# Attention into a mixture of experts: relu of k and a share of the v scaling on GpSimd, relu of q as one operation, a first block table of six batches

## The chip, the cores and the metric

The kernel runs on one core of one Trainium2 chip. Its time is device microseconds of one execution. The core has five engines that take instructions from queues of their own, each in order: TensorE (PE, whose weight loads are listed as PEld), VectorE (DVE), ScalarE (ACT), GpSimd (POOL) and SyncE (SP, which here only issues DMAs). Engines wait for each other by semaphores only.

## The reference

q, k and v are 8 batches x 8 heads x 576 tokens x 64, in float32. The attention is linear, so there is no 576 x 576 matrix; its output is the input of a mixture of 8 experts in which each token goes to one expert.

```python
phi(x) = concat(relu(x) * cos(theta), relu(x) * sin(theta))     # theta = pi/2 * pos / 576
kv  = einsum('bhsf,bhsd->bhfd', phi(k), v);  z = sum_s phi(k)
x   = (phi(q) @ kv) / (phi(q) @ z + 1e-6)                       # 4608 tokens x 512
e   = argmax(x @ w_gate);  gate = softmax(x @ w_gate)[e]
y   = relu(x_of_expert @ w1[e]) @ w2[e]                         # 512 -> 1024 -> 512, at most 1152 tokens an expert
out[token] = gate * y
```

## The kernel before

**Attention, batch by batch.** A batch is 576 tokens of 8 heads, held as two halves u of four heads. SP loads k, q (one transfer a half) and v. Relu of k is done in place (`relu_k`, L408 to L416: two ACT operations of 128x1152 a batch). Instead of scaling k by cos and sin, the kernel scales v (`scale_v`, L421 to L436): for each of nine position groups j and each of the two tables one operation of 128x256, those of odd j on ACT (8 a batch), those of even j on DVE (10 a batch). Relu of q (`q_relu`, L441 to L446) goes from the loaded layout (head, j, 64) to a layout in which PE can transpose two heads at a time (j, head, 64); it is four DVE operations of 128x576 a batch, one for each half and head of a pair. Then come, per batch:

- KV (L491, PE): 2 x 36 matmuls; needs relu of k and all 18 scaled v pieces.
- Q (L454, PE, three groups a half) with copies to SBUF by ACT (`rq`, L461).
- kvt (L503, ACT), T (L520, PE), tsb (L525, ACT), G (L534, PE), kva (L508 and L539, ACT): the gate weights are folded into KV, so that x @ w_gate comes out of the same matmuls as x.
- P (L561, PE): ten units a batch; each is followed by a copy (`tmp`, L568, ACT) and a scalar_tensor_tensor (`num`, L573, DVE). Three PSUM slots ("p") hold them.

**Routing of a batch.** A chain of some 20 small DVE operations (L614 to L722) finds each token's expert and gate; in the middle stands a group of small matmuls on PE (L680 to L687, called "count" below) that counts tokens, with a running sum (`carry`, L698) from batch to batch. Five pieces of the tokens (`xg`, L745; two on POOL, three on DVE) are scaled, cast to bf16 and scattered by POOL's indirect DMAs (L754, five a batch) into `xd` in DRAM, where each expert has a region.

**Block tables and the experts.** The experts work on 43 blocks of 128 rows of `xd`. Two tables say which expert and which row each block has. Table a (`tab_ops`, L784 to L892, some 18 DVE operations) is made from the carry after BA = 7 batches and holds the NA = 24 blocks that are certain to be full by then; table b holds the NB = 19 others, after batch 8. SP makes a small read of `xd` (`seen`, L1066) that waits for the scatters of the first BA batches; every fetch of a block (`xr`, L948) comes after it. Fetches of table b's blocks also wait for the last scatters and for eight DMAs of zeros that ACT issues (`pad`, L882). A block is: fetch, transpose by PE (L957), copy to `un` by DVE (L961), up-projection half 0 (L977, `w1a`), relu (L984, ACT), transpose (L992), copy (L998, DVE); later half 1 (`w1b`) the same way, and last the down-projection (L1018), a copy (L1024 ACT or L1026 DVE) and POOL's scatter to the output (L1035). PE's order is: all half-0 blocks, all half-1 blocks, all down blocks, with some mixing at the seams. Weights are loaded by POOL's DMAs (L899, L910); w1a during the attention, the others after `swap` has given the attention's memory to them.

**What sets the order.** A planner in the kernel (`Plan.schedule`, L87) takes each operation with an engine, a cost and a latency, and a priority to which the table `PHI` adds an offset by name. It makes one list; each engine gets its operations in that order and keeps to it, whatever happens on the chip. So a changed cost or offset moves instructions on all engines.

Of the kernel before, what the change touches and what calls it, by code (L numbers as in the profile page):

```python
# [27 lines left out]
    "G": -1.04, "KV": -0.66, "P": -0.87, "R": -0.81, "T": -0.03, "carry": 0.36, "down": -0.02, "end": 1.83,  # L28
    "gout": -0.99, "hT": -1.51, "ids": -0.3, "ix": 0.26, "kva": -0.29, "kvt": -1.41, "load": 0.03, "pad": 1.0,
    "pos": -0.09, "relu": 0.27, "reluk": -0.58, "reluq": -0.46, "rq": -0.61, "scat": 1.16, "tab": 1.94,  # L30
    "tmp": 0.1, "tsb": -2.25, "turn": -0.08, "up": 0.59, "vs": -1.24, "w1": 1.29, "w2": 1.39, "wg": 0.98,
    "xT": -0.23, "xg": 1.25, "xturn": 1.8, "y": 0.55,
# [141 lines left out]
def kernel(  # L174
# [30 lines left out]
    BA = 7  # L205
# [4 lines left out]
    U0, U1, U2 = 4, 41, 42  # L210

# [191 lines left out]
    def attention(b):  # L403
# [4 lines left out]
        def relu_k(u):  # L408
            def f():
                kk = loaded[b, "k", u].tile[:]  # L410
                nc.scalar.activation(out=kk, in_=kk, func=ACT.Relu)  # L411
            return f

        for u in range(2):
            op("ACT", 1.1, relu_k(u), r=[("k", b, u)], w=[("rk", b, u)], vers=[loaded[b, "k", u]], prio=pr - 0.4,
               ).tag = ("reluk", b, u)  # L416
# [4 lines left out]
        def scale_v(j, t):  # L421
            def f():
                tab = (cosn, sinn)[t]
                dst, src = vs_t[vs.slot][:, :, j, t, 0:D], vm.tile[:, :, j, :]
                if (j, t) in ON_ACT:
                    nc.scalar.activation(out=dst, in_=src, func=ACT.Copy, scale=tab[:, j:j + 1])
                else:
                    nc.vector.tensor_scalar(out=dst, in0=src, scalar1=tab[:, j:j + 1], scalar2=None, op0=ALU.mult)
            return f

        ON_ACT = {(j, t) for j in range(J) for t in range(2) if j % 2}
        for j in range(J):
            for t in range(2):
                act = (j, t) in ON_ACT
                op("ACT" if act else "DVE", 0.41 if act else 0.31, scale_v(j, t), r=[("v", b, 0), ("v", b, 1)],
                   w=[("vs", b, j)], vers=[vs, vm], prio=pr - 0.3).tag = ("vs", b, j, t)  # L436
# [4 lines left out]
        def q_relu(u, qr, c):  # L441
            def f():
                t = tl(qr, [P, J, 2, D], FP32, "early")
                nc.vector.tensor_scalar(out=t[:, :, c, :], in0=loaded[b, "q", u].tile[:, c, :, :], scalar1=0.0,  # L444
                                        scalar2=None, op0=ALU.max)
# [19 lines left out]
        for u in range(2):  # L465
            qr = Ver(qrS)
            for c in range(2):
                op("DVE", 0.38, q_relu(u, qr, c), r=[("q", b, u)], w=[("qr", b, u)], vers=[loaded[b, "q", u], qr],
                   prio=pr - 0.4).tag = ("reluq", b, u, c)
            for jq in range(3):  # L470
# [3 lines left out]
                op("PE", 0.11 * n, f, r=[("qr", b, u)], w=[("qps", b, u, jq)], vers=[pv, rq[u], qr], prio=pr,  # L474
                   mode="full").tag = ("Q", b, u, jq)
                op("ACT", 0.5 if n == 4 else 0.22, g, r=[("qps", b, u, jq)], w=[("rq", b, u)], vers=[pv, rq[u]],
                   prio=pr - 0.2).tag = ("rq", b, u, jq)
# [19 lines left out]
        for u in range(2):  # L497
            op("PE", 2.07, kv_half(u), r=[("rk", b, u)] + [("vs", b, j) for j in range(J)], w=[("kvps", b)],
               vers=[kv, kva, loaded[b, "k", u], vs], prio=pr, mode="quad").tag = ("KV", b, u)
# [11 lines left out]
        op("ACT", 0.52, kvt_out, r=[("kvps", b)], w=[("kvt", b)], vers=[kv, kvt], prio=pr - 0.5).tag = ("kvt", b)  # L511
        op("ACT", 0.53, kva_out, r=[("kvps", b)], w=[("kva", b)], vers=[kv, kva], prio=pr - 0.5).tag = ("kva", b)
# [30 lines left out]
        op("PE", 0.45, transp, r=[("kvt", b)], w=[("tps", b)], vers=[tv, tsb, kvt], prio=pr - 0.5, mode="full").tag = ("T", b)  # L543
# [607 lines left out]
```

## Time and profile before

| what | value |
|---|---|
| median of 3 runs (lowest, highest) | 405.65 us (404.07, 406.15) |
| the profiled execution, its span | 407.73 us, 406.0 us |
| busy: PE, DVE, ACT, POOL | 329.1, 215.0, 178.0, 143.3 us |
| attention on PE (first KV to last P) | 10.45 to 176.2 us |
| first up-projection | 197.72 us |
| first down-projection | 323.74 us |
| mean TensorE clock | 0.931 |

The profile page has the span in 40 slices of about 10.15 us, with a digit for the busy tenths of each engine, and the clock that TensorE was granted (PEclk). The stage table used below gives for each stretch its length and then each engine's busy us and instruction count in the order PE, PEld, DVE, ACT, POOL, and last the clock, the busy share of the DMA engines and GB/s. Group lines give: line, engine, operation, output and inputs with their shapes, count, busy us, mean ns, and what the engine waited for before them. Lines about one source line give the duration of one as shortest/median/longest in ns.

### The profile page before, as it was taken

The numbers are of one execution on the slowest core, as the hardware profiler recorded it, in microseconds if no ns is written. First come the engines' busy times: TensorE is split into PE (matmuls) and PEld (weight loads), VectorE is DVE, ScalarE is ACT, GpSimd is POOL, SyncE is SP. The second block draws the span as 40 slices with busy tenths as digits, with TensorE's granted clock in tenths as the row PEclk, the third lists the DMA queues.
The fourth block names the chain that finished last, engine by engine and source line by source line (L and its number), as shares of the span: only waits on it lengthen the run. The fifth ranks groups of instructions, "written<-read, shape, count | busy, mean of one in ns | idle before, by whom it ended". The sixth has DMA issues, their size and how long they took to land.

```text
span 406.0 us, 9624 instructions
## 1 busy us (share of the span) xinstructions
PE 329.1 (81%) x3333; PEld 218.0 (54%) x3356; DVE 215.0 (53%) x612; ACT 178.0 (44%) x369; POOL 143.3 (35%) x212
## 2 busy tenths in 40 slices
PE   0886788898969799830587779899999999999992
PEld 0776676687757588620344345555555544444440
DVE  7548988876938758789543344454333322222220
ACT  6359787866737653620132324334555411111110
POOL 3001627153441604575423211215000046556552
PEclk9989999969988959985599999999999999999997
DMA  8975979699680530529999995645960024433320
GB/s 293 360 284 184 329 260 307 199 269 254 194 241 19 178 52 16 98 69 189 219 193 231 193 197 123 140 115 94 210 114 0 2 105 155 152 149 129 136 104 10
DMA packets 39535, 66.63 MB, mean 164 GB/s; under 512 B 4927, under 2 KB 19647, under 8 KB 39490
## 3 DMA queue, kind: packets, MB, share of 16 engines
q0 software_dynamic: 18032, 30.96, 34.6%
q1 hardware_dynamic: 20306, 34.01, 25.3%
q10 hardware_dynamic: 1152, 1.05, 0.8%
q8 instruction: 29, 0.48, 0.5%
q14 instruction: 16, 0.13, 0.1%
HBM read 67.56 MB, written 17.06 MB: 208 GB/s over the span
## 4 chain that ended last, share of the span: by engine, by line
PE 51%; DVE 14%; issue 9%; DMA 8%; POOL 7%; ACT 7%; another core or an unknown queue 2%; POOLq 1%; SPq 0%; DVEq 0%; ACTq 0%
PE p L977 18%; PE p L1018 9%; PE p L561 9%; POOL out_dram L1035 5%; PE a L992 4%; PE a L454 3%; DMA wg_n<-in_moe_w_gate_dram 3%; DMA xr<-xd 2%; PE a L957 2%; DVE qr L444 2%; DVE xg L745 2%; PE p L491 2%; PE a L534 2%; DVE num L573 2%; DMA km<-in_k_dram 2%
## 5 line engine op out<-in xcount | busy, mean ns | idle before, releaser
L984 ACT ACTIVATE h<-p 128x512 bf16<-128x512 f32 x86 | 51.3, 597 | 92.8 <-PE p L977 55.4
L1018 PE MATMUL p<-w,un 128*128 x337 | 74.2, 379 | 0.4
L998 DVE COPY un<-a 128x512 bf16<-128x512 bf16 x86 | 36.2, 423 | 62.4 <-PE a L992 62.1
L561 PE MATMUL p<-kva,rq 64*128 64x146 f32 x640 | 58.6, 326 | 8.0 <-DVE num L573 5.1
L561 PEld LDWEIGHTS p<-kva,rq 64*128 64x128 f32 x640 | 49.2, 212 | 15.3 <-DVE num L573 7.1
L573 DVE SCALAR_TENSOR_TENSOR num<-p,tant,tmp 128x292 f32<-128x292 f32 (+1 forms) x80 | 39.2, 512 | 33.6 <-ACT tmp L568 29.5
L1018 PEld LDWEIGHTS <-un 128*128 128x128 bf16 x344 | 33.6, 98 | 40.3 <-issue 0.4
L491 PE MATMUL p<-vs,km 64*64 64x130 f32 x1152 | 41.0, 286 | 14.7 <-ACT km L411 12.2
L977 PEld LDWEIGHTS <-un 128*128 128x128 bf16 x344 | 32.6, 98 | 33.7 <-issue 8.8
L754 POOL DMA_INDIRECT xd<-xg,si x40 | 42.9, 1074 | 21.4 <-DVE xg L745 12.3
L977 PE MATMUL p<-w1a,un 128*128 x162 | 44.1, 392 | 7.0 <-DVE un L961 4.4
L568 ACT COPY tmp<-p 128x292 f32<-128x292 f32 (+1 forms) x80 | 31.4, 401 | 33.3 <-PE p L561 21.3
L1026 DVE COPY y<-p 128x512 f32<-128x512 f32 x22 | 15.2, 691 | 57.7 <-PE p L1018 46.0
L491 PEld LDWEIGHTS p<-vs,km 64*64 64x64 f32 x1152 | 35.8, 141 | 18.6 <-issue 14.8
L1035 POOL DMA_INDIRECT out_dram<-y,ids x24 | 23.6, 982 | 60.2 <-issue 60.2
L977 PE MATMUL p<-w1b,un 128*128 x166 | 43.3, 377 | 0.4
L992 PEld LDWEIGHTS <-h 128*128 128x128 bf16 x344 | 25.2, 98 | 26.2 <-ACT h L984 10.5
L1024 ACT COPY y<-p 128x512 f32<-128x512 f32 x21 | 12.3, 585 | 60.9 <-PE p L1018 57.9
L992 PE MATMUL a<-identb,h 128*128 128x128 bf16 x344 | 33.1, 220 | 6.0 <-ACT h L984 3.5
L957 PE MATMUL a<-identb,xr 128*128 128x128 bf16 x172 | 17.5, 227 | 14.9 <-DMA xr<-xd 11.6
L454 PE MATMUL a<-ident,qr 128*128 128x128 f32 x144 | 26.7, 313 | 2.1 <-ACT rq L461 0.9
L952 POOL COPY ids<-xr 128x2 bf16<-128x2 bf16 x43 | 7.8, 189 | 57.7 <-DMA xr<-xd 57.4
(157 smaller groups left out, 384.4 us busy)
## 6 DMA issues: line engine op xcount, KB each, us to landing
vm<-in_v_dram SPq DMA_DIRECT2D x16, 576.0 KB
km<-in_k_dram SPq DMA_DIRECT2D x16, 576.0 KB
qm<-in_q_dram SPq DMA_DIRECT2D x16, 576.0 KB
w<-in_moe_w_dram POOLq DMA_DIRECT2D x16, 512.0 KB
xr<-xd SPq DMA_DIRECT2D x43, 128.5 KB
w1a<-in_moe_w_dram POOLq DMA_DIRECT2D x8, 512.0 KB
w1b<-in_moe_w_dram POOLq DMA_DIRECT2D x8, 512.0 KB
xd<-zrow ACTq DMA_DIRECT2D x8, 128.5 KB
```

What stands on the lines that cost most here:

```text
L454: nc.tensor.transpose(out=q_ps[:, n * P:(n + 1) * P], in_=qr.tile[:, j, :, :].rearrange("p c d -> p (c d)"), identity=ident[:])
L491: nc.tensor.matmul(out=kv_v[c * D:(c + 1) * D, o, u, :, :], lhsT=loaded[b, "k", u].tile[o * D:(o + 1) * D, c, j, :], rhs=vs_t[vs.slot][o * ...
L561: nc.tensor.matmul(out=p_ps[:, a, o, 0:2 * KW], lhsT=rq[u].tile[a * D:(a + 1) * D, o, col:col + P], rhs=kva.tile[a * D:(a + 1) * D, o, u, ...
L568: nc.scalar.copy(out=t[0:rows], in_=p_v[0:rows, :, 0:KW])
L573: nc.vector.scalar_tensor_tensor(out=num.tile[0:rows, c, u * HB:(u + 1) * HB, :], in0=p_v[0:rows, :, KW:2 * KW], scalar=tant[0:rows, c:c + ...
L754: si = nc.gpsimd.indirect_dma_start(out=xd[:, :], out_offset=bass.IndirectOffsetOnAxis(ap=xg.si[0:rows, c:c + 1], axis=0), in_=xg.tile[0:r ...
L977: nc.tensor.matmul(out=hp, lhsT=xv.tile[:, g, :], rhs=w1h[m][:, bass.ds(e1, 1), g, :], start=(g == 0), stop=(g == G - 1))
L984: nc.scalar.activation(out=h[:], in_=pvs[m].tile[:, 0, :].rearrange("p (g q i) -> p g i q", g=2, i=2), func=ACT.Relu)
L992: nc.tensor.transpose(out=t_ps[:, x * P:(x + 1) * P], in_=hvs[m].tile[:, x // 2, x % 2, :], identity=identb[:])
L998: nc.vector.tensor_copy(out=unit(hts[m])[:].rearrange("p f s -> p (f s)"), in_=tvs[m].tile[:].bitcast(BF16)[:, 0:512])
L1018: nc.tensor.matmul(out=y_ps, lhsT=hts[x // G].tile[:, x % G, :], rhs=w2h[x // G][:, bass.ds(e2, 1), x % G, :], start=(x == 0), stop=(x == ...
L1035: oi = nc.gpsimd.indirect_dma_start(out=out[:, :], out_offset=bass.IndirectOffsetOnAxis(ap=idx, axis=0), in_=yv.tile[:], in_offset=None, b ...
```

## The change

1. Relu of k goes from ACT to POOL (16 operations of 128x1152; `tensor_scalar` with max).
2. Of the v scaling, j = 4 and j = 8 go from DVE to POOL (32 operations of 128x256); DVE keeps six a batch, ACT its eight.
3. Relu of q is one DVE operation for each half (16 in all, in place of 32): it reads 2 x 9 x 64 in the loaded order and writes to the same target layout, the head as outermost dimension.
4. BA = 6 in place of 7, so table a has 20 blocks and table b 23. Three scratch tiles of the two tables (`sq`, `ge`, `gm`) become shared.
5. For the first 14 blocks the copy after the fetch's transpose goes from DVE to ACT (`XT_ACT`).
6. The w1a loads are released earlier: load e after KV of batch 3e/4, where it was e + 1.
7. The planner's costs, latencies and the whole table `PHI` are new.

```diff
 PHI = {
...
+    "G": 8.78, "KV": 6.99, "P": -1.6, "R": 1.52, "T": -0.09, "down": -0.82, "fetch": -0.06, "hT": -0.31,
...
-    BA = 7
+    BA = 6
...
+    XT_ACT = 14
...
-                nc.scalar.activation(out=kk, in_=kk, func=ACT.Relu)
+                nc.gpsimd.tensor_scalar(out=kk, in0=kk, scalar1=0.0, scalar2=None, op0=ALU.max)
...
+                    eng = nc.vector if where == "DVE" else nc.gpsimd
+                    eng.tensor_scalar(out=dst, in0=src, scalar1=tab[:, j:j + 1], scalar2=None, op0=ALU.mult)
...
-        ON_ACT = {(j, t) for j in range(J) for t in range(2) if j % 2}
+        def vs_on(j, t):
+            return "ACT" if j % 2 else "POOL" if j in (4, 8) else "DVE"
...
-                nc.vector.tensor_scalar(out=t[:, :, c, :], in0=loaded[b, "q", u].tile[:, c, :, :], scalar1=0.0,
-                                        scalar2=None, op0=ALU.max)
+                nc.vector.tensor_scalar(out=t[:].rearrange("p j c d -> p c j d"), in0=loaded[b, "q", u].tile[:],
+                                        scalar1=0.0, scalar2=None, op0=ALU.max)
...
+            if name not in T and name in ("sq", "ge", "gm"):
+                if name not in wide:
+                    m = E if name == "sq" else max(NA, NB)
+                    wide[name] = late.tile([P, m, shape[2]], dt, name=name)
+                T[name] = wide[name][:, 0:shape[1], :]
...
-            nc.vector.tensor_copy(out=unit(xv)[:].rearrange("p g s -> p (g s)"),
-                                  in_=xpv.tile[:].bitcast(BF16)[:, 0:DT])
+            dst, src = unit(xv)[:].rearrange("p g s -> p (g s)"), xpv.tile[:].bitcast(BF16)[:, 0:DT]
+            if i < XT_ACT:
+                nc.scalar.copy(out=dst, in_=src)
+            else:
+                nc.vector.tensor_copy(out=dst, in_=src)
...
-        w1_load(0, e, e + 0.1, ops_of("KV", min(e + 1, B - 1)))
+        w1_load(0, e, e + 0.1, ops_of("KV", 3 * e // 4))
```

## The prediction

> **What bounds the kernel now.** I read the slices of the page first, for where PE stands still, then the table by stage, then the timeline of the standstill, then PE's waits inside the attention.
>
> ```profile
> PE   0886788898969799830587779899999999999992
> PEclk9989999969988959985599999999999999999997
> 25.00:176.30 151.30, 127.85 (x1962) 107.50 (x1959) 115.59 (x313) 101.80 (x236) 59.93 (x66) 0.92 0.63 182
> 176.30:197.70 21.40, 1.79 (x23) 1.28 (x23) 18.91 (x69) 0.63 (x2) 15.12 (x21) 0.58 0.84 180
> 197.70:204.80 7.10, 6.87 (x31) 3.62 (x32) 1.70 (x4) 1.79 (x3) 0.64 (x3) 0.60 1.00 187
> 204.80:270.00 65.20, 52.98 (x415) 30.25 (x422) 28.09 (x84) 22.09 (x37) 15.09 (x48) 1.00 0.86 176
> 323.70:399.00 75.30, 74.26 (x341) 33.78 (x347) 15.81 (x24) 12.72 (x22) 41.15 (x42) 1.00 0.34 127
> ```
>
> From 204.8 us on PE works nearly all the time, and 75.3 us at the end are down-projections at full rate: nothing in the change touches them. There are two places to gain. The first is the hole at 176.3 us: 21.4 us with PE busy 1.8. The timeline shows what fills it: table a's 18 operations on DVE (182.67 to 187.87, for batch 8's routing comes first), the read "seen" (188.66), the first fetch (189.72), its transpose, and ACT's zero DMAs beside it.
>
> ```profile
> 188.66 0.33 SPq L1069 DMA_DIRECT2D seen<-xd  x1
> 191.39 7.92 ACTq L882 DMA_DIRECT2D xd<-zrow  x8
> 192.07 0.61 PE L957 MATMUL a<-identb,xr 128*128 128x128 bf16 x4 [11.05 <-DMA xr<-xd]
> ```
>
> The second is the attention. The counts of the routing (L680) start at 38.66, 59.31, 77.80, 104.51, 128.78, 152.33 and 167.59 us: 6 intervals of 21.5 us a batch. In the row from 25 to 176.3, PE is idle for 151.3 - 127.85 = 23.4 us, and the clock of 0.92 costs about 0.08 x 151.3 = 12 us more: 3.3 and 1.7 us a batch, which leaves 16.5 us of PE work. The idle time has these owners:
>
> ```profile
> PE p L561 <- DVE num L573: 5.1, 6, 1.7
> PE a L534 <- ACT tsb L525: 4.3, 5, 2.6
> PE a L520 <- ACT kvt L503: 2.8, 2, 2.4
> PE p L491 <- ACT km L411: 1.7, 1, 1.7
> ```
>
> All are late copies on DVE and ACT. The two longest (2.4 us at 117, 2.6 us at 142) stand beside the stretches in which PEclk falls to about half.
>
> **The hole (items 4, 6, 7).** In the built program's order, table a now stands on DVE right behind the sixth count, and PE still has, from that count to the last P: 20 P (1.26 us for two: 12.6), two KV halves (2.23 each: 4.5), T 0.66, two G (2.2), six Q groups (2.4), a count (0.6): 23 us. The other path from the same count: table 5 us (its time now), rest of the routing 2.3, POOL's two xg pieces 2.06, five scatters of 1.28 apart (6.4), landing 2.7, "seen" 1.0, fetch and landing 2.4: 22 us. They tie; I take 1.5 us of waiting for the first fetch in place of 21.4.
>
> What is late next: the eight zero DMAs took 7.92 us of ACT in the hole, at no cost. In the new order they stand in ACT's queue behind the fifth relu of the experts and ahead of the eighth copy of item 5 (`un7`) and the sixth relu. They wait for the eighth count, which itself comes a num (0.5), three xg pieces (2.0) and nine DVE operations (3.1 us) after the last P. PE has five up blocks by then (5 x 1.3 = 6.5 us, plus the start), and three or four things after; ACT is busy till about 17 us after the last P. Cost: 7 us of idle PE, plus about 3 us of low clock after it (the row at 0.60 shows four blocks in 7.1 us where 1.3 us each do, start to start, at 254 to 262 us). That low clock at the start, 3 us, is gone now, since PE comes straight from the attention. Sum: -21.4 + 1.5 + 7 + 3 - 3 = **-13 us**, between -19 (the zero DMAs hidden) and -7 (first fetch 6 us late).
>
> Fetches of table b need the last scatters and the zero DMAs, some 24 us after the last P; 20 blocks of table a at 1.3 us or more reach to 26: free. Item 5 moves 14 x 0.42 us (L961) to ACT at 0.59 (L1024's row): ACT then has 1.2 us a block against PE's 1.3 to 1.7; free, behind the zero DMAs. The shared scratch joins operations that are in order on DVE anyway: nothing. The earlier w1a loads put two more of 512 KB into the attention, whose DMA share is 0.63: nothing.
>
> **The attention (items 1, 2, 3, 7).**
>
> ```profile
> L411 ACT ACTIVATE km<-km x16: 1144/1164/1187, 9.2 to 146.9; 128x1152 f32<-128x1152 f32 x16
> L444 DVE TENSOR_SCALAR qr<-qm x32: 733/743/753, 11.6 to 159.1; 128x576 f32<-128x576 f32 x32
> L428 DVE TENSOR_SCALAR vs<-vm,sinn x40: 335/346/652, 7.4 to 152.4; 128x256 f32<-128x256 f32 x40
> L745 POOL TENSOR_TENSOR xg<-num,rden x16: 1039/1050/1053, 42.7 to 183.8; 128x512 bf16<-128x512 f32 x16
> L736 POOL TENSOR_SCALAR xg<-tok_i x8: 222/236/1789, 5.4 to 168.3; 128x5 int32<-128x5 int32 x8
> L808 DVE TENSOR_SCALAR cia<-cia x1: 1052/1052/1052, 182.9 to 182.9; 128x8 int32<-128x8 int32 x1
> L808 DVE TENSOR_SCALAR cib<-cib x1: 172/172/172, 190.7 to 190.7; 128x8 int32<-128x8 int32 x1
> ```
>
> *ACT* loses 16 x 1.164 = 18.6 us: 2.3 a batch.
>
> *POOL* gains 16 relus and 32 scalings, which the trace does not show. Nearest above: the xg row with two inputs, 2.05 ns an element, so 2.4 us for 1152. Nearest below: POOL's memset of 64x584, 650 ns, against 100 for one of a single element: 0.94 ns an element, 1.2 us. An operation with one input is nearer to the memset: 1.2 us, and 0.4 (0.34 to 0.52) for 256. POOL gets 4 us a batch (6.9 at most), on about 8.5 now (59.93 us over 7 batches) and 1.5 of gaps between scatters: 14 of 21.5.
>
> *DVE* loses 32 scalings at 0.265 (eight in a row took 2.22 us): 8.5 us. The joined relu lies between L444's rate (1.04 ns an element: 1.3 us, no gain on 2 x 0.66 from start to start) and twice that, at which L428 seems to run: at L444's rate its 256 elements would take 0.41, and it takes 0.35. L428's outermost extent is even (four heads), as is the joined relu's (two), and L444's is nine, so I take 0.75: 16 x 0.57 = 9 us (0 to 10). If it stays at the slow rate, those 9 us stay away, which at half weight makes the forecast 383. Together 17 us, 2.2 a batch.
>
> Against this speaks that DVE and POOL hold each other up. L808 takes 1052 ns beside POOL's xg and 172 without; L736 takes 1789 ns in the middle of a burst of L428 and 236 without. L428 has a tail, L444 none. The new 32 us of POOL lie over some 20 DVE operations a batch of the kinds that can be hit: 13% of the time under a relu with 0.6 us left on the mean, 8% under a scaling with 0.2: 1.9 us a batch, 15 us in all at worst, and nothing if they rarely meet. Of the Trainium skill, "SBUF — State Buffer", section "Who interferes with whom", says that a two-port VectorE operation and a GpSimd operation lock each other out for a whole instruction; the rows above agree. By that rule the joined relu becomes such an operation, and as an estimate the whole 15 us would be paid and DVE's gain would shrink to 2 us.
>
> So DVE's gain is near nothing to 17, ACT's is firm, and the new order puts other work between kvt, T, tsb and G, where PE waited 7.1 us. Of the idle 23.4 us I take half (11.7), of the 12 us of clock a third (4), less 2 for the holding up: **-14 us**, 19.2 us a batch. Ends: all of both, -35; and +4, half a microsecond a batch of holding up without a gain.
>
> **Sum.** 406.0 - 13 - 14 = 379 us of span, 380.7 for the execution (407.73 now). The profiled execution lies 2.1 us above the median, so 379 against 405.65.
>
> **Rivals.**
> - *Only the hole goes.* DVE and POOL hold each other up for as much as DVE and ACT give, and batches stay at 21.5 us: 405.65 - 13 = 393. For it: the tail of L736, and that DVE is the busiest engine after PE in this stage (115.59); against it: ACT's 18.6 us don't depend on it.
> - *The order does more.* PE never waits long enough for the clock to fall: -26 in the attention, 367. For it: the last two counts now are 15.3 us apart, with the clock up; against it: DVE still has some 15 us a batch.
> - *POOL becomes the bound, slower than before.* Relu of k stands in POOL's queue with scatters behind it, and table a's fetch waits for the sixth batch's scatters. If each of the six new operations a batch waits 1.9 us (L736 waited 1.55 once), POOL needs 10 + 4 + 11.4 = 25.4 us a batch; 6 x 3.9 = 23 us longer, less 13: 416. It decides from 1.4 us a wait (13 us longer).
> - *The first fetch doesn't tie.* If the sixth batch's scatters slip by 10 us, the hole is half there: 389; it lies in the range.
>
> **Chances.** Forecast (373 to 388) 0.48; only the hole (388 to 400) 0.24, with the late fetch; the order does more (360 to 373) 0.19; POOL the bound 0.09, of which 0.06 slower. A change below 0.5% (2 us) can't be told from none here: 0.02. So faster 0.92, same 0.02, slower 0.06. The range of 8 in 10 takes the forecast, most of the next two: 364 to 398.
>
> **What would show it.** The hole: the first x transpose within 3 us of the last P; then 5 to 8 us of idle PE about 10 us after it, with ACT on zero DMAs. POOL's relu at 1.2 us, the joined q relu near 0.75 but with a tail. The counts 18 to 20 us apart. Wrong would be a POOL relu over 2.4 us, counts over 21.5 us apart, or idle PE ahead of KV that ends with POOL.

## The result and the profile after

The changed kernel takes 425.20 us (median of 4 runs, 424.08 to 427.18) against 405.90 us for the kernel before on the same chip (4 runs, 404.07 to 409.17): a ratio of 1.047, interval 1.039 to 1.055. It is slower; the forecast was 379 us. The profiled execution took 424.08 us, its span is 422.0 us and its mean TensorE clock 0.915. Some executions are in a slower state of the chip; the medians in this document contain them and the ratios and intervals do not, so a ratio is not always the quotient of two medians.

First PE's two rows of slices in the page of the changed kernel, then the stage table, with the columns as before.

```profile
PE   0757969497786839498737986899999999999992
PEclk9977888859699879689997999999999999999998
```

```profile
25.00:206.00 181.00, 134.88 (x1970) 117.20 (x1968) 145.18 (x291) 86.77 (x219) 135.76 (x110) 0.83 0.56 159
206.00:215.00 9.00, 7.48 (x65) 4.44 (x67) 6.95 (x24) 6.05 (x12) 5.69 (x10) 1.00 0.79 168
215.00:223.00 8.00, 0.08 (x2) 0.00 (x0) 7.42 (x22) 0.56 (x2) 6.44 (x6) 0.83 1.06 239
```

The stage from 25 us to just after the last P is now 181 us long where it was 151.3. In it PE is idle for 46.1 us (23.4 before), POOL is busy for 135.8 us (59.9 before), and the clock is down from 0.92 to 0.83. The first seven counts start 24.4 us apart (21.5 before). The old hole is gone: the row from 206 has PE at work straight away. A shorter one has come instead, at 215 us. In the timeline of PE and ACT there:

```profile
204.91 0.62 PE L965 MATMUL a<-identb,xr 128*128 128x128 bf16 x8
214.87 7.54 ACTq L890 DMA_DIRECT2D xd<-zrow  x8
223.08 0.58 PE L965 MATMUL a<-identb,xr 128*128 128x128 bf16 x4 [8.00 <-ACT un L971]
```

The last P ends at 205.0 us (176.2 before). The first x transposes of the experts follow on it without a wait, and 10 us later PE stands for 8.00 us behind a copy that waits behind ACT's zero DMAs. That is what was forecast for this part. The operations that were moved, as shortest/median/longest ns:

```profile
L411 POOL TENSOR_SCALAR km<-km x16: 3104/3148/3194, 8.8 to 149.1; 128x1152 f32<-128x1152 f32 x16
L430 POOL TENSOR_SCALAR vs<-vm,cosn x16: 913/964/1795, 5.9 to 160.3; 128x256 f32<-128x256 f32 x16
L430 DVE TENSOR_SCALAR vs<-vm,cosn x24: 312/448/8135, 7.6 to 161.0; 128x256 f32<-128x256 f32 x24
L447 DVE TENSOR_SCALAR qr<-qm x16: 740/751/4160, 12.9 to 189.9; 128x1152 f32<-128x1152 f32 x16
L616 DVE TENSOR_TENSOR rden<-num,epsc x8: 203/224/6336, 43.1 to 208.4; 128x40 f32<-128x40 f32 x8
L747 POOL TENSOR_TENSOR xg<-num,rden x16: 1048/1491/1551, 55.9 to 217.0; 128x512 bf16<-128x512 f32 x16
```

POOL's relu takes 3.15 us, where ACT's took 1.164 and the forecast had 1.2; its scaling takes 0.96. And operations of DVE that need 0.2 to 0.75 us by themselves have a longest case of 4 to 8 us. DVE does 58 operations fewer and is busy 27 us longer (242.1, before 215.0). What such a case is, POOL's and DVE's timelines show at 67 us:

```profile
67.10 9.37 POOL L411 TENSOR_SCALAR km<-km 128x1152 f32<-128x1152 f32 x3
```

```profile
68.49 8.13 DVE L430 TENSOR_SCALAR vs<-vm,cosn 128x256 f32<-128x256 f32 x1
76.55 0.93 DVE L575 SCALAR_TENSOR_TENSOR num<-p,tant,tmp 128x292 f32<-128x292 f32 x2
```

Three relus run on POOL without a gap, and one 0.35 us scaling on DVE ends when they end. Behind it in DVE's queue stand the two `num` for which PE's P waits, and behind those the batch's routing. PE's waits from 20 to 215 us say the same:

```profile
PE p L563 <- DVE num L575: 22.5, 9, 6.7
PE a L522 <- ACT kvt L505: 5.7, 1, 5.7
PE a L682 <- DVE oh L649: 5.1, 1, 5.1
```

The wait for `num` was 5.1 us in six pieces; it is now 22.5 in nine, one of them 6.7 long.

### The profile page after: what moved, and what is told of

It reads as the page before. It is cut to its first block, busy times and chain, and to the rows that moved or that the text cites. A ratio compares the mean times of both kernels' runs of the same rounds, so it can differ in the third digit from the quotient of the medians.

```text
span 422.0 us, 9628 instructions
## 1 busy us (share of the span) xinstructions
PE 333.4 (79%) x3333; PEld 225.3 (53%) x3356; DVE 242.1 (57%) x554; ACT 168.9 (40%) x367; POOL 232.1 (55%) x260
## 3 DMA queue, kind: packets, MB, share of 16 engines
q1 hardware_dynamic: 20306, 34.01, 24.2%
q10 hardware_dynamic: 1152, 1.05, 0.9%
## 4 chain that ended last, share of the span: by engine, by line
PE 44%; DVE 22%; POOL 8%; issue 8%; DMA 8%; ACT 3%; another core or an unknown queue 2%; SPq 1%; ACTq 1%; POOLq 1%; DVEq 0%
PE p L988 16%; PE p L1029 8%; PE p L563 8%; DVE vs L430 6%; POOL out_dram L1046 5%; DMA xr<-xd 4%; PE a L1003 4%; DVE xg L747 3%; DVE num L575 3%; DMA vm<-in_v_dram 3%; PE p L493 3%; POOL km L411 2%; PE a L457 2%; DVE qr L447 2%; DVE rden L616 2%
## 5 line engine op out<-in xcount | busy, mean ns | idle before, releaser
L563 PE MATMUL p<-kva,rq 64*128 64x146 f32 x640 | 62.4, 352 | 23.3 <-DVE num L575 22.5
L563 PEld LDWEIGHTS p<-kva,rq 64*128 64x128 f32 x640 | 55.0, 236 | 29.5 <-DVE num L575 26.6
L493 PE MATMUL p<-vs,km 64*64 64x130 f32 x1152 | 42.3, 297 | 13.5 <-POOL km L411 12.0
L1046 POOL DMA_INDIRECT out_dram<-y,ids x20 | 19.5, 977 | 57.1 <-DVE y L1037 45.4
L756 POOL DMA_INDIRECT xd<-xg,si x40 | 44.5, 1112 | 11.1 <-issue 7.1
L411 POOL TENSOR_SCALAR km<-km 128x1152 f32<-128x1152 f32 x16 | 50.0, 3145 | 0.6 <-DMA km<-in_k_dram 0.5
L570 ACT COPY tmp<-p 128x292 f32<-128x292 f32 (+1 forms) x80 | 31.3, 401 | 46.1 <-PE p L563 35.3
L1037 DVE COPY y<-p 128x512 f32<-128x512 f32 x22 | 15.2, 691 | 57.7 <-PE p L1029 49.4
L493 PEld LDWEIGHTS p<-vs,km 64*64 64x64 f32 x1152 | 37.3, 148 | 17.0 <-POOL km L411 12.0
L1003 PE MATMUL a<-identb,h 128*128 128x128 bf16 x344 | 32.4, 219 | 4.1 <-ACT h L995 3.5
L1046 POOL DMA_INDIRECT out_dram<-y,ix x23 | 22.3, 970 | 17.1 <-DVE y L1037 10.1
```

What stands on the lines that cost most here:

```text
L411: nc.gpsimd.tensor_scalar(out=kk, in0=kk, scalar1=0.0, scalar2=None, op0=ALU.max)
L493: nc.tensor.matmul(out=kv_v[c * D:(c + 1) * D, o, u, :, :], lhsT=loaded[b, "k", u].tile[o * D:(o + 1) * D, c, j, :], rhs=vs_t[vs.slot][o * ...
L563: nc.tensor.matmul(out=p_ps[:, a, o, 0:2 * KW], lhsT=rq[u].tile[a * D:(a + 1) * D, o, col:col + P], rhs=kva.tile[a * D:(a + 1) * D, o, u, ...
L570: nc.scalar.copy(out=t[0:rows], in_=p_v[0:rows, :, 0:KW])
L756: si = nc.gpsimd.indirect_dma_start(out=xd[:, :], out_offset=bass.IndirectOffsetOnAxis(ap=xg.si[0:rows, c:c + 1], axis=0), in_=xg.tile[0:r ...
L1003: nc.tensor.transpose(out=t_ps[:, x * P:(x + 1) * P], in_=hvs[m].tile[:, x // 2, x % 2, :], identity=identb[:])
```

## The experiments

The theory after the result: relu of k on POOL is the loss, by its length and by what stands behind it. Rivals: the scaling on POOL; the joined relu of q; the new order. The runs fell into five groups, each on another chip. The kernel before took 386.28, 384.01, 384.26 and 385.71 us on the first four of them and 406.53 on the fifth, so ratios to it within a group are compared, and microseconds only within a group or where the text says so.

| kernel | median us | ratio to before, interval |
|---|---|---|
| changed kernel again (a2) | 416.24 | 1.082 (1.074, 1.089) |
| relu of k on ACT (e1) | 378.54 | 0.980 (0.972, 0.988) |
| scaling on DVE (e2) | 415.98 | 1.078 (1.071, 1.086) |
| both given back (e3) | 383.19 | 0.983 (0.974, 0.992) |
| before, relu of k on POOL (e4) | 425.63 | 1.109 (1.101, 1.118) |
| 27 memsets for the relu (e8) | 391.09 | 1.019 (1.013, 1.024) |
| relu in four pieces (e9) | 405.80 | 1.056 (1.049, 1.062) |
| 102 memsets for the relu (e10) | 405.22 | 1.053 (1.048, 1.057) |
| planner with true costs (e11) | 423.82 | 1.105 (1.097, 1.113) |
| e1, zero DMAs on SP (e6) | 378.51 | 0.986 (0.981, 0.991) |
| `gate` on DVE (e12) | 418.88 | 1.086 (1.076, 1.097) |
| relu in pieces, `gate` on DVE (e13) | 398.94 | 1.035 (1.025, 1.045) |
| e1, relu of q in two (e15) | 384.62 | 0.994 (0.990, 0.999) |
| before, table of six (e14) | 386.86 | 1.003 (0.998, 1.008) |
| e14, copies on ACT (e16) | 417.12 | 1.025 (1.020, 1.029) |
| e16, joined relu of q (e17) | 401.63 | 0.987 (0.983, 0.992) |

**Single operations (m1).** Each operation alone, three or more in a row, then kinds of DVE operations beside six of POOL's relus:

```python
G.tensor_scalar(out=ko[:], in0=kf, scalar1=0.0, scalar2=None, op0=ALU.max)      # POOL, 6 in a row
V.tensor_scalar(out=qr[:].rearrange("p j c d -> p c j d"), in0=qm[:], ...)       # DVE beside them, 12
```

> A kernel of single operations, none of the reference's work: GpSimd's relu and scaling alone, then the same relu beside one kind of VectorE operation at a time. If the price is GpSimd's own, relu of 128x1152 takes about 3.1 us and scaling of 128x256 about 0.9 us with nothing beside them. If the price comes from the two engines holding each other up, they take 1.2 and 0.4 us alone. Beside the relu: the split relu of q (128x576) keeps its 0.74 us, the joined relu, the scaling and the 128x40 product with two inputs in SBUF are stretched to up to 3 us each, about one of them for each relu.

In the groups of this kernel, L57 is POOL's relu alone, L66 the scaling, L72 a copy, L74 a product with two inputs, L78 a memset; L92 is the split relu of q beside POOL's relu, L97 the joined one, L95 POOL's relu beside that, L102 DVE's scaling beside POOL's relu, L107 a product of 128x40:

```profile
L57 POOL TENSOR_SCALAR ko<-kk x3: 3114/3114/3115, 4.7 to 11.1; 128x1152 f32<-128x1152 f32 x3
L66 POOL TENSOR_SCALAR vo<-vm,tab x3: 922/923/928, 33.0 to 34.8; 128x256 f32<-128x256 f32 x3
L72 POOL COPY ko<-kk x3: 1142/1142/1146, 41.4 to 43.8; 128x1152 f32<-128x1152 f32 x3
L74 POOL TENSOR_TENSOR ko<-kk,kz x3: 2607/2608/2608, 45.1 to 50.4; 128x1152 f32<-128x1152 f32 x3
L78 POOL MEMSET ko<- x3: 1057/1057/1057, 57.1 to 59.4; 128x1152 f32 x3
L92 DVE TENSOR_SCALAR qs<-qm x14: 743/753/754, 69.2 to 79.4; 128x576 f32<-128x576 f32 x14
L97 DVE TENSOR_SCALAR qr<-qm x12: 759/2152/3580, 88.4 to 113.9; 128x1152 f32<-128x1152 f32 x12
L95 POOL TENSOR_SCALAR ko<-kk x6: 3115/3496/3497, 88.2 to 105.7; 128x1152 f32<-128x1152 f32 x6
L102 DVE TENSOR_SCALAR dv<-vm,tab x18: 335/342/3276, 115.0 to 136.9; 128x256 f32<-128x256 f32 x18
L107 DVE TENSOR_TENSOR so<-sm,kz x18: 199/199/2928, 137.7 to 157.7; 128x40 f32<-128x40 f32 x18
```

The 3.11 us are the relu's own; nothing ran beside it. It is slower than a product with two inputs (2.61), and takes 2.7 times as long as a copy of the same size (1.14), about what the forecast put it at (1.2, from a memset). And the split relu is untouched beside it (0.754 at most), while the joined relu, the scaling (3.276 at most) and a two-input product of 0.2 us wait for a whole relu. None of them waits for more than one, though six relus stand in a row on POOL: the longest is 3.580 us. In the changed kernel one waited through the rest of three (8.13 us). What makes this difference no run here shows.

**Which of the two moves (e1, e2, e3).** The order of the changed kernel is kept, only the engine that is issued to differs:

```diff
-                nc.gpsimd.tensor_scalar(out=kk, in0=kk, scalar1=0.0, scalar2=None, op0=ALU.max)
+                nc.scalar.activation(out=kk, in_=kk, func=ACT.Relu)          # e1 and e3
...
-                    eng = nc.vector if where == "DVE" else nc.gpsimd
+                    eng = nc.vector                                          # e2 and e3
```

> The changed kernel with relu of k given back to ACT, at the same place in the order. Theory A (GpSimd's queue is full: relu 3.15 us, scaling 0.95 us): GpSimd loses 50 us, the attention falls back below 180 us, total 385 to 395. Theory B (VectorE is held up by GpSimd's long operations): the same total, and VectorE's stretched operations (scaling up to 8 us) go. Rival C (the new order of the instructions is to blame): stays above 410.

> The changed kernel with the v scaling of j = 4 and 8 given back to VectorE, at the same place in the order; relu of k stays on GpSimd. Theory A: GpSimd loses 32 us of 232, total 405 to 415. Theory B: VectorE gets 32 operations more that can be held up and loses 32 short holds: 412 to 425. Rival C: no change, 425.

> The changed kernel with both given back, the order as in the changed kernel, the joined relu of q and the table of six batches kept. Theories A and B: the prediction's sum without its POOL terms, 375 to 388. Rival C: above 406. The first block's transpose within 3 us of the last P, the idle stretch behind the zero DMAs 6 to 8 us in any case.

Relu of k is the loss. With it back on ACT the kernel is faster than the one before, 0.980; with only the scaling back it stays at 1.078, so the rival that the scaling is the loss falls. The scaling on POOL neither gains nor costs anything that can be told: 0.980 with it and 0.983 without. In e1 DVE is busy 201.0 us, 41 less than in the changed kernel (242.1), and its longest scaling is short again:

```profile
L430 DVE TENSOR_SCALAR vs<-vm,cosn x24: 315/360/583, 7.3 to 121.7; 128x256 f32<-128x256 f32 x24
```

**The same move in the old order (e4, b2, a2).** e4 is the kernel before with relu of k on POOL (the first line pair above, the other way round); b2 and a2 are both kernels profiled on the second chip.

> The kernel before with one edit, relu of k on POOL in place of ACT, at the place in the program that ACT's relu has; scaling, relu of q, order and block tables are the old ones. If moving relu of k is by itself the loss: 3.15 us each, 50 us more on POOL, VectorE's scalings and two-input products longer than in the kernel before, POOL's small `gate` later: 396 to 415, ratio 1.03 to 1.08. Rival: the operation costs little by itself and the loss lies in where the new order puts it: within 1.5% of the kernel before.

> The kernel before, profiled on the chip on which the variants of the changed kernel ran (386.28 us there, 405.65 on the first), to see which part of the expected gain was there to be had. If the first chip's 20 us more were clock and waits of PE in the attention: counts of the routing about 19 us apart (21.5 on the first chip), less than 15 us of idle PE between the first count and the last P (23.4), and the hole before the experts unchanged at 20 to 22 us. If instead the hole is shorter here, the small gain of the variant with relu of k on ACT (378.54) comes from there.

> The changed kernel beside the others of this call. With relu of k on ACT it took 378.54, with the scaling on DVE 415.98, both against 386.28 for the kernel before. Both theories (POOL's queue time, or DVE held up under POOL's operations) expect it near the second of these: 408 to 420, ratio 1.055 to 1.09.

The move costs 11% without any of the rest, more than the 3 to 8% expected, so the new order isn't needed to make it costly; within the new order it cost about 10% (1.082 against 0.980). The two are not quite the same loss. A part of e4's lies at the start, in the timelines of PE and POOL:

```profile
24.12 5.82 PE L491 MATMUL p<-vs,km 64*64 64x130 f32 x144 [24.12 <-POOL km L411]
```

```profile
20.12 0.75 POOL L325 COPY wg_sb<-wg_n 64x32 f32<-64x32 f32 x4 [14.37 <-DMA wg_n<-in_moe_w_gate_dram]
20.95 12.37 POOL L411 TENSOR_SCALAR km<-km 128x1152 f32<-128x1152 f32 x4
```

POOL's first relu stands behind copies that wait for a load of w_gate, so the first KV starts at 24.12 us where it starts at 10.47 in b2. By the first count 6.5 us of that are left (46.51, 40.0); by the last P e4 is 36.9 us late (193.0, 156.1; the two chips take 384.26 and 384.01 us for the kernel before). The other 30 us come between, and there DVE is shut out as in the changed kernel: its longest scaling takes 6.97 us, under two relus. Nor is the joined relu of q needed for the loss: e4 has the split one, which takes 0.753 us at most. In b2 the hole is as it was (21 us, one wait of 11.5 us for the first fetch in it; span 384.5 us), but the attention is shorter than on the first chip: its counts are 17.9 us apart (21.5 there), at a clock of 0.96 over 25 to 157 us (0.92).

**By which way relu on POOL costs (e8 to e10, e12, e13).** Two ways were in question: DVE is shut out while POOL works (B), or work stands behind the relu in POOL's queue (A).

```diff
+                for n in range(BURN):                       # e8: 27, between two tiny relus; e10: 102
+                    nc.gpsimd.memset(burn[:, n:n + 1], 0.0)
+                nc.scalar.activation(out=kk, in_=kk, func=ACT.Relu)
...
+                for n in range(0, 1152, 288):               # e9 and e13
+                    nc.gpsimd.tensor_scalar(out=flat[:, n:n + 288], in0=flat[:, n:n + 288], scalar1=0.0, ...)
...
-            nc.gpsimd.tensor_scalar(out=rv["gate"][:], in0=rv["gate"][:], scalar1=1e-9, scalar2=None, op0=ALU.add)
+            nc.vector.tensor_scalar(out=rv["gate"][:], in0=rv["gate"][:], scalar1=1e-9, scalar2=None, op0=ALU.add)  # e12, e13
```

> The changed kernel with relu of k on ACT, and in relu's place on POOL a tiny relu of one element per partition (already relu'd again by ACT, so the values are those of the reference), 27 memsets of one element per partition (0.1 us each) and the tiny relu again: POOL's queue is occupied as long as by the 3.1 us relu and KV waits for its end, but no single operation of it is long. Theory A (POOL's queue time: scatters, xg and KV stand behind the relu) expects about the time of the changed kernel or a little more, 408 to 425, since ACT's 1.16 us comes on top. Theory B (a relu of 3.1 us holds up VectorE's operations for its whole length) expects nearly the time with relu on ACT: 378 to 390, POOL as busy as in the changed kernel, VectorE's scalings and joined relus back at 0.34 and 0.75 us. Half way (395) would mean that both count.

> The changed kernel with POOL's relu of k cut into four operations of 288 elements (0.92 us each by the measured singles: 3.70 us in place of 3.11). Theory A expects 0.6 us more for each of 16 relus on a queue that is the bound: 3 to 9 us slower than the changed kernel. Theory B expects an operation of VectorE to wait for one piece instead of a whole relu, unless POOL goes straight on to the next piece ahead of it: waits of VectorE of 3 us and more become 0.9, and the kernel is 8 to 20 us faster than the changed one.

e8 was ill built and tells neither: the memsets started 31 ns apart, not 105, so that POOL was occupied for 1.1 to 1.6 us each time in place of 3.1, and ACT's relu now waited 10.7 us for POOL. e9 is 10 us faster than the changed kernel (1.056 and 1.082, intervals apart) although POOL's 64 pieces take 63.2 us where the 16 whole ones took 50.6. DVE is busy 207.8 us (245.2 in a2): most of the shutting out has gone, the longest scaling being 3.03 us. But DVE stands elsewhere. POOL's and DVE's timelines of e9, at the place shown above for the changed kernel:

```profile
66.83 8.99 POOL L413 TENSOR_SCALAR km<-km 128x288 f32<-128x288 f32 x9
75.81 0.93 POOL L433 TENSOR_SCALAR vs<-vm,cosn 128x256 f32<-128x256 f32 x1
76.73 0.92 POOL L433 TENSOR_SCALAR vs<-vm,sinn 128x256 f32<-128x256 f32 x1
77.63 0.91 POOL L433 TENSOR_SCALAR vs<-vm,cosn 128x256 f32<-128x256 f32 x1
78.63 0.24 POOL L659 TENSOR_SCALAR gate<-gate 128x5 f32<-128x5 f32 x1
```

```profile
69.32 0.39 DVE L433 TENSOR_SCALAR vs<-vm,sinn 128x256 f32<-128x256 f32 x1
78.90 0.19 DVE L662 RECIPROCAL gate<-gate 128x5 f32<-128x5 f32 x1 [9.19 <-POOL gate L659]
```

DVE got through its work by 69.7 us and then waits 9.19 us for `gate`, an operation of 0.24 us that stands on POOL between two of DVE's, behind the rest of three relus and three scalings. Such waits add up to 31.3 us in e9, and to 1.8 in a2, where DVE is late for the same reason earlier on.

> The changed kernel with relu of k on ACT, which waits for nothing of POOL, and in relu's place in POOL's queue 102 memsets of one element per partition. In the run with 27 memsets they started 31 ns apart, so 102 take 3.1 us, and POOL is as busy as in the changed kernel. Theory A (queue: `gate`, xg and scatters stand behind the relu, and VectorE waits in order for `gate`) expects 395 to 410, ratio 1.03 to 1.07, with VectorE idle 15 to 30 us ahead of the reciprocal that follows `gate`. Theory B (only a long operation that shuts VectorE out costs) expects the time with relu on ACT, 376 to 384, ratio 0.98 to 1.0.

> The changed kernel with one small operation a batch moved from POOL to VectorE: `gate` (128x5, 0.23 us), which stands on POOL between two operations of VectorE. VectorE then never waits for POOL's queue in its routing. If VectorE's being shut out under relu is a cost by itself: 408 to 418, ratio 1.06 to 1.09, since in the changed kernel VectorE is idle only 1.8 us ahead of the reciprocal that follows `gate`. If shutting out and waiting at `gate` are one and the same loss, the second being hidden under the first, there is nothing more to gain here either. A time under 400 would mean that `gate` is what costs.

> Relu of k on POOL in four pieces, which in the run before left VectorE unhindered (207.8 us busy, 245.2 with whole relus) but idle for 31.3 us ahead of the reciprocal that follows `gate`, and `gate` on VectorE. If the two ways in which VectorE comes to stand behind POOL are the whole loss, it is gone with both: 378 to 388, ratio 0.98 to 1.01. If POOL itself is the bound (xg and scatters late, 63 us of relu in its queue): 395 to 406, ratio 1.03 to 1.055.

e10 came out where theory A had it (405.2), but not purely: DVE waited 9.2 us for `gate`, where 15 to 30 were expected, and its joined relu also lengthened beside the memsets (longest 5.06 us, 24.2 us in all against 12.1 in e1), so a queue of tiny operations shuts DVE out as well. In e12 `gate` alone is on DVE, and nothing is gained (1.086 and 1.082, intervals overlap): the waits for `gate` lie behind the shutting out. With both taken away, in e13, the ratio is 1.035. That lies in the second of the two ranges expected, for POOL itself as the bound: about half of the distance between the changed kernel (1.082) and e1 (0.980) is gone. Among PE's waits in the attention of e13 are, beside 3.3 us for `oh`:

```profile
PE a L525 <- DVE pos L706: 10.0, 1, 10.0
PE p L496 <- POOL km L413: 7.3, 3, 6.0
PE p L566 <- DVE num L578: 6.1, 9, 1.4
PE p L496 <- POOL vs L433: 2.6, 2, 2.3
```

KV waits for relu and scaling on POOL for 9.9 us here, behind the start none in the changed kernel; the `num` wait, 22.5 us there, is back at 6.1. The longest, 10.0 us for `pos`, leads to POOL as well, by way of the loads. From the timelines of POOL, SP and DVE:

```profile
91.38 9.24 POOL L413 TENSOR_SCALAR km<-km 128x288 f32<-128x288 f32 x8
100.61 0.93 POOL L433 TENSOR_SCALAR vs<-vm,cosn 128x256 f32<-128x256 f32 x1
101.53 0.92 POOL L433 TENSOR_SCALAR vs<-vm,sinn 128x256 f32<-128x256 f32 x1
102.47 0.88 SPq L398 DMA_DIRECT2D vm<-in_v_dram  x2
103.97 1.36 SPq L398 DMA_DIRECT2D qm<-in_q_dram  x2
116.01 0.87 DVE L450 TENSOR_SCALAR qr<-qm 128x1152 f32<-128x1152 f32 x1 [11.58 <-DMA qm<-in_q_dram]
```

SP stood 13.4 us ahead of the two v loads until POOL, behind eight pieces of relu, had scaled out of v; the q loads stood behind them, DVE waited 11.58 us for q, and `pos` stood behind that relu of q. The attention of e13 loses to e1 mainly in two of its intervals between counts: first to second 29.0 us (21.6 in e1), in which KV waits 7.0 us for relu, and fourth to fifth 32.4 us (21.3), in which this wait lies. In neither does PE wait for a scatter. This is one trace.

**The planner with true costs (e11).**

```diff
-            op("POOL", 1.2, relu_k(u), ...
+            op("POOL", 3.15, relu_k(u), ...
...
-                op(where, {"ACT": 0.4, "DVE": 0.3, "POOL": 0.4}[where], scale_v(j, t), ...
+                op(where, {"ACT": 0.4, "DVE": 0.3, "POOL": 0.95}[where], scale_v(j, t), ...
```

> The changed kernel with two numbers of its planner set to what the trace shows: 3.15 us for POOL's relu (1.2), 0.95 for its scaling (0.4). The operations are the same ones, in another order: in the old plan up to three relus stand ahead of a batch's `gate` on POOL, in this one two at most. If the order made with wrong costs is a part of the loss: 395 to 410, ratio 1.03 to 1.065. If the operation costs it wherever it stands: within 1% of the changed kernel, ratio 1.07 to 1.09.

1.105, above both ranges and slower than with the false costs. In its order relus run on POOL while DVE is in the chain of the routing: `dl`, a difference of 128x40 in that chain that takes 0.2 us by itself, takes up to 6.67 us and 16.8 us in eight (1.7 in a2), and PE waits 22.4 us in five pieces for `oh`, which stands behind it and ahead of the count. The planner has no notion that an operation on POOL stops DVE, and a right duration didn't help it.

**The zero DMAs on SP (e6).**

```diff
-                zi = nc.scalar.dma_start(out=xd[bass.ds(r0, P), :], in_=zrow[:])
+                zi = nc.sync.dma_start(out=xd[bass.ds(r0, P), :], in_=zrow[:])      # on top of e1
```

> The changed kernel with relu of k on ACT (378.5) and the eight zero DMAs issued by SP in place of ACT; in the program they stand between SP's ninth and tenth fetch. If the 8.3 us that ACT waited for `end` on behalf of the zero DMAs are what stopped PE for 7.9 us: 7 to 9 us less, 369 to 373, ratio 0.955 to 0.97, and no idle PE behind `un`. Rival: the fetches that now stand behind the zero DMAs on SP's queue come late, and PE waits for them instead: 375 to 380, ratio 0.97 to 0.985.

No gain: 0.986, and e1 0.980, intervals overlapping. PE's 7.9 us behind ACT's copy are gone. In their place PE stands 5.35 us for a copy on DVE, and its granted clock is 0.50 from 180.3 to 187 us. In the timeline of e6:

```profile
170.91 0.38 PE L965 MATMUL a<-identb,xr 128*128 128x128 bf16 x4 [0.67 <-ACT un L971]
180.34 2.11 PE L1003 MATMUL a<-identb,h 128*128 128x128 bf16 x16 [5.35 <-DVE un L1009]
184.17 0.61 PE L965 MATMUL a<-identb,xr 128*128 128x128 bf16 x4 [1.05 <-DMA xr<-xd]
```

DVE had three xg pieces (3.60 us from 170.59) and some 20 operations of table b ahead of that copy, and SP's next fetch stood behind the zero DMAs. The time lies in the rival's range, but the wait that took the place of the first is mainly DVE's copy, and for a fetch only 1.05 us. Two waits lay side by side, and taking one left the other.

**What the rest of the change gives (e15, e14, e16, e17).** e15 is e1 with relu of q in two operations per half again. e14 is the kernel before with the table of six batches and the shared scratch alone; e16 adds the copies on ACT (`XT_ACT = 14`), e17 also the joined relu of q. None of the last three touches relu of k or the scaling, and all use the old `PHI`. In e17 the planner has one entry for a relu of q in place of two, so its order may shift too.

```diff
-    BA = 7
+    BA = 6                                                  # e14, e16, e17
...
+            if i < XT_ACT:
+                nc.scalar.copy(out=dst, in_=src)            # e16, e17
...
+                nc.vector.tensor_scalar(out=t[:].rearrange("p j c d -> p c j d"), in0=loaded[b, "q", u].tile[:], ...)   # e17
```

> The changed kernel with relu of k on ACT (378.5) and relu of q in two operations per half again: 16 x 0.7 = 11 us more on VectorE, which works 109 of the 135 us from 20 to 155 there. If VectorE's work is on the path (PE waits 7.7 us for num): 381 to 388, ratio 0.99 to 1.01. If it isn't: 377 to 381, ratio 0.975 to 0.99.

> The kernel before with the first block table of six batches alone (and the shared scratch that it needs), ordered by the old planner settings: none of the other changes. The changed kernel with relu of k back on ACT ends its experts' part 13 us earlier than the kernel before, but its last count comes 5 us later, as the new order's first count does. If the table is what gains, and the new order of the attention what gives 5 us back: 367 to 374, ratio 0.955 to 0.975. Rival: the table needs the new planner settings, without which PE waits for `seen` and the first fetch as before: 380 to 386.

> The kernel before with the block table of six batches and with the copies after the first 14 fetches' transposes on ACT, in the old planner settings; nothing of relu or scaling. With the table alone the first fetch came 6 us earlier than in the kernel before, but PE then waited 8.4 us for one of these copies, which stood on VectorE behind table work and the routing. If that wait is what ate the table's gain: 6 to 10 us faster than before, 376 to 380, ratio 0.974 to 0.985. Rival: ACT then waits for `end` on behalf of its zero DMAs with copies behind it, as in the changed kernel, and the gain stays away: 384 to 388, ratio 0.995 to 1.005.

> As the kernel with the table and the copies on ACT, and relu of q as one operation per half too: all of the change that doesn't use POOL, in the old planner settings. In the new order the joined relu was worth 6 us (378.5 with relu of k on ACT, 384.6 with two operations per half as well). If it is worth as much in the old order: 4 to 8 us less than without it, 369 to 375, ratio 0.957 to 0.975, and the fastest kernel of this study. Rival: the old order has VectorE's work off the path, and nothing changes: within 1% of the kernel without it.

The joined relu of q gains: 0.994 without it and 0.980 with it in the new order (different groups, intervals a hair apart), and 1.025 without and 0.987 with it in the old one, in the same group. There the last count starts at 170.01 us in e17 and at 181.84 in e16, 11.8 us earlier. The table alone gains nothing (1.003). e14, e16 and e17 all came out above the ranges expected of the theory, e16 above its rival's too. The waits of PE in e14 (its profiled execution took 390.45 us and its median is 386.86, so the sizes are rough):

```profile
166.65 0.61 PE L962 MATMUL a<-identb,xr 128*128 128x128 bf16 x4 [5.42 <-DMA xr<-xd]
178.23 0.58 PE L982 MATMUL p<-w1a,un 128*128 x1 [8.35 <-DVE un L966]
```

PE waits 6 us less for the first fetch than in b2 (5.42 against 11.49), and then the first up block waits 8.35 us for a copy on DVE. With the copy on ACT (e16) PE waits 8.61 us for it there, because ACT's eight zero DMAs stand ahead of it; the whole is slower than before, 1.025. With the new order the first fetch has landed by the time the last P ends: in e1 the first x transposes start at 157.49 us, right behind the last P, in e14 at 166.65, 10.2 us behind it. It is not the copies or the joined relu that bring this, for in e17 they start 9.1 us behind it (174.93, 165.81); nor the moves to POOL, for in e3 they start right behind it (161.04). What is left is the planner's settings and the earlier w1a loads, which no run tells apart. From the last P to the end b2 needs 228.4 us and e1 219.1.

## Why the prediction was wrong

**The step that failed is the price of POOL's operations**: "An operation with one input is nearer to the memset: 1.2 us, and 0.4 (0.34 to 0.52) for 256". Measured: 3.11 and 0.92 us alone, 3.15 and 0.96 in the kernel. Both bounds were taken from operations of other kinds, and the upper one (2.4 us, a product with two inputs) holds only if fewer inputs can't be slower; m1 shows that they can (3.11 us with one, 2.61 with two). By these durations POOL gets 6.3 us of relu and 3.8 of scaling a batch, 10.1 in place of 4. Two of the prediction's own signs of being wrong came: a relu over 2.4 us on POOL (3.15), and counts over 21.5 us apart (24.4).

**The holding up was mis-sized with it.** It was put at "1.9 us a batch, 15 us in all at worst", from a relu of 1.2 us that an operation meets half way, and it entered the sum with 2 us. A relu is 2.6 times as long, they stand two and three in a row on POOL, and one operation lost nearly 8 us under three of them. DVE is busy 44 us longer in a2 than in e1 (245.2, 201.0), 5.5 us a batch. The rule cited from the Trainium skill, "SBUF — State Buffer", section "Who interferes with whom", spoke against this change; the forecast kept 2 of the 15 us that it would cost by that rule. m1 agrees with it: the split relu, which has no tail in the trace of before either, isn't touched, and the joined one, the scaling and a product with both inputs in SBUF are shut out for a whole operation (3.580, 3.276 and 2.928 us at the longest).

**The rival "POOL becomes the bound, slower than before"** (416, at 0.09) came nearest, with 425 us. It was to decide from 1.4 us of additional time for each new operation, 8.4 us a batch; by their own durations the six take 2 x 1.95 + 4 x 0.56 = 6.1 us more than priced, and the rest of the loss came through DVE. POOL was not full either: it is busy for 135.8 of the 181 us of the attention's row. So its mechanism, scatters standing behind relu, is at most a part. DVE being shut out, DVE waiting for `gate`, and KV waiting for relu are three places where the same lateness of POOL shows; taking away the first gave 10 us (a2 to e9, the same group), the second after it about 8 (1.056 to 1.035 of 385 us), and the second alone nothing. The `gate` operation on POOL between two of DVE's was in the trace of before, and the prediction does not name it as a place where DVE waits for POOL's queue. Of the remaining half, e13's trace puts the two largest pieces down to relu and scaling on POOL that are late for KV and for the loads; that taking these away too would bring back all of e1's time was not tried.

**The hole** was right. Forecast: -13 us, with 7 us of idle PE behind the zero DMAs. Measured from the last P to the end of the span: 229.8 us before and 217.0 after, -12.8; idle 8.0 us. That the sum agrees to 0.2 us is luck, for its terms don't: the first fetch cost nothing in place of 1.5 us, and the idle time is 1 us longer. The tie of first fetch and last P held in the slow attention, and in the fast one of e1 and e3 too. What e14, e16 and e17 add is that this gain doesn't come from the table alone: without the new order other waits take its place.

**The attention** was to give 14 us and lost 28.8 on the first chip (last P at 205.0 in place of 176.2). Relu on POOL does not explain all of that shortfall. With relu back on ACT, and so without the 18.6 us that ACT was to save, the attention gains nothing either: the last P ends at 157.6 us in e1 and 161.1 in e3, against 156.1 in b2. The counts of e1 are 17.5 us apart against 17.9, but the first comes 5.0 us later. So all that e1 has is the 9.3 us of the experts' part. What ACT's saving would have been worth if relu had cost 1.2 us on POOL no run shows. There was also less to gain: PE was idle for 15.2 us in b2's stage from 25 to 157 us, with the clock at 0.96, where the forecast reckoned with 23.4 us and 0.92. The joined relu of q was right in time (0.75 us) and in size (9 us expected; 6 by e15 and e1, 15 by e16 and e17, 11.8 of them in the attention), as long as no relu on POOL stands beside it. The scaling's 8.5 us on DVE bought nothing: e1 has DVE busy only 4.4 us less than e3 (201.0, 205.4), in part since the scalings that it keeps lengthen from a mean of 0.36 to 0.43 us, and the time is the same. In the new order the xg pieces lengthen each other: in e3, without any of the moves to POOL, one on POOL takes 1.40 us (1.05 in b2) and one of 64 rows on DVE 1.10 (0.67). What that costs in all is not shown.

**The chances.** 0.06 on slower was too little for a forecast whose largest unknown, an operation that no row showed, went into a queue with an engine behind it. A range drawn from bounds that aren't bounds can't hold.

The fastest kernel of the study is the changed one with relu of k on ACT, 0.980 (0.972 to 0.988); e3, e6 and e17 are not told apart from it by their intervals.

## What to carry to other kernels

Price an operation that moves to another engine by the same kind of operation on that engine, and if the trace has none, measure it alone before anything else: a copy or a memset of the same size says little about a `tensor_scalar` (1.14 and 1.06 against 3.11 us on POOL). Before long work goes onto POOL, list what DVE has to wait for in POOL's queue, however small, and which DVE operations have a form that POOL shuts out; one of them can stand through several POOL operations in a row (8.13 us here), and a `num` or routing step behind it pays. When one wait on a seam is removed, look for the one beside it (zero DMAs, copies, table work here): in e6 and e16 another took its place.

## What the runs showed of the hardware

- POOL, alone, on 128x1152 float32: relu by `tensor_scalar` 3.114 us, product of two tiles 2.608, copy 1.142, memset 1.057. Cut pieces cost 1.643 us for 576 and 0.924 for 288 elements: four quarters are 19% longer than the whole.
- Whether a DVE relu is shut out goes with its form. Beside POOL's relu, 128x576 read as nine positions took 0.754 us at most, and 128x1152 with the outermost extent two 3.580; alone both take 0.75 us, so the joined form does twice the work in the time. DVE's scaling, with an outermost extent of four, is shut out too (3.276).
- How long differs: beside six relus in a row in m1 no DVE operation took over 3.580 us, while in the kernel one took 8.13 under three. Why stays open.
- It goes both ways: POOL's relu took 3.496 us beside joined relus, and 3.115 beside split ones.
- POOL starts memsets of one element per partition 31 ns apart though each is listed with 105 ns on the mean (e8; 115 in e10); the 16 x 102 = 1632 of e10 occupied it for 49.8 us.
- The same kernel took 384 to 386 us on four chips and 406 on two, at mean clocks of 0.946 (b2) and 0.931.
